# A fused scan and feed-forward kernel: another written order of its opening (loads, weights, early up-projections, PSUM banks)

## The chip, the core and the metric

The kernel runs on one core of a Trainium2 chip. The core has a matrix engine (PE, with its weight loads shown as PEld), a vector engine (DVE), a scalar engine (ACT), a general engine (POOL) and a queue engine (SP) that here only issues DMAs. Each takes its own instructions in order; DMAs are issued from SP, from ACT and from POOL. The metric is the time of one execution on the device in microseconds (us); less is better. The compared number is the median of several executions.

## The reference

Two layers run one after the other. The first is a state-space scan over x (4 batches, 8 heads, 768 steps, 32 wide) with decays a, and B and C (16 states); the second is a feed-forward layer with squared ReLU on the 3072 tokens of 256 features that come out of it.

```python
for c in range(nc):                                   # 24 chunks of 32 steps
    cum = np.cumsum(log(clip(a, 1e-6, 1))[chunk])
    L = np.exp(cum[:, None] - cum[None, :]) * causal
    M = (Cc @ Bc.T) * L                               # scores, masked and decayed
    y[chunk] = M @ xc + (Cc @ state) * np.exp(cum)    # inside the chunk + carried state
    state = np.exp(sum(la)) * state + (Bc * np.exp(cum[-1] - cum)).T @ xc
h = np.maximum(x @ w_in, 0.0)                         # x: y as (3072, 256); w_in (256, 2048)
out = h * h @ w_out                                   # w_out (2048, 256)
```

## The kernel before

The work is cut into twelve units of 256 steps, one per batch and third of the sequence: units 0 to 3 are the first thirds of the four batches, 4 to 7 the second, 8 to 11 the last. Inside a unit the scan is done in two halves of 128 steps. A unit goes through: loads of C, B and x; products with running decay products P and 1/P (`prep_c`, `prep_b`, `prep_x`, lines 152 to 181: C times P and a cast of B into the tile `jt`, x over P into `xs`); a transpose of `jt` on PE (L195) and its copy to `bct` (L208 on ACT, L210 on DVE); scores on PE (`ph_mt`, L220) into PSUM banks 0 to 3; the causal mask on each of the four banks (L229 on DVE directly, or L234, a copy on ACT, and then L238 on POOL or DVE); state products (`ph_u`) and the products inside the unit and with the carried state (`ph_carry`, `ph_intra`; all through the helper's L245); and a copy of the result from PSUM to the tile T (`ph_t`), which is already the transposed input of the feed-forward layer. For the units of the first thirds the state that goes from the first half of the unit to its second is built from PSUM in one instruction, Sd (`ph_sd_first`, L343).

The feed-forward work of a unit is called a block, a to l for units 0 to 11. It has eight up-projections (`mm1`, L403, four matmuls each into one PSUM bank, and L408, the ReLU on ACT), eight squares (L414, on DVE) and eight down-projections (`mm2`, L430, four matmuls each into the block's accumulator in bank 6 or 7). Up-projection f of any block needs the f/2-th of four loads of w_in, down-projection f the f/2-th of four loads of w_out. These eight loads are issued from POOL and convert from 32 to 16 bits on the way (L139, L143).

P comes from a: two loads of 16 KB each for the first thirds (units 0 to 3) and one of 64 KB for the rest, a clip and a scan on DVE (L468, L469), then products on PE that spread the result over partitions (L452, and L521 or L537 for the totals of a half), read from PSUM bank 4 by the first unit and copied to `P_sb` for the others (L688). `Ptot` and `Pquad` (L524, L527) hold the totals. The second and last thirds have a scan of their own (`second_scan`, L468, L469, L532) and products of their own (`second_p`).

The order of all instructions is written out by hand in the string ORDER (lines 48 to 69), token by token; `one` (L655) turns a token into calls, and each engine takes its own instructions in that order. Tokens used below: `fa0`, `fa1`, `la` the loads of a; `ldC0:l:a` a load of C for unit 0, here its first four heads, from ACT's queue (`s` SP; without `l` or `h` all eight heads); `wi0`, `wo0` weight loads; `gB3`, `afC2` instructions on POOL that touch a loaded tile; `ef eb ti ku pi` constants on POOL; `sk` the first scan, `sp` L452, `su` L521, `ps` and `to` the copies of P and of the totals, `fq` L527, `sn`, `p2`, `pq` the same for the other thirds; `pc pb px` the preparations, `tr tc` transpose and copy, `mt` scores, `mk` a direct mask, `sc` and `ms` a copied one, `u` state products, `sf` Sd, `ina inb in` and `ca` products inside and from the carried state, `t` the copy to T, `us` a copy of the state, `zb sb` the state after a unit; `a0` to `l7` up-projections, `qa0` squares, `A0` down-projections; `id3:512` three filler matmuls of 512 columns (L476).

PSUM banks are handed out by `bank` and `pair`, the longest unused one first. Where fillers stand, PE has nothing else to do in that order. DMAs issued from SP and ACT take eight completion semaphores in turn, so a load waits until the one eight places before it has landed.

## Time and profile before

| | |
|---|---|
| median of 3 runs | 116.54 us (116.23 to 118.86) |
| the profiled execution's own time | 116.84 us |
| span of its profile, first to last instruction | 115.1 us |
| PE, PEld, DVE, ACT, POOL busy | 108.9, 93.5, 84.2, 76.7, 49.8 us |
| chain that ended last | PE 87%, DMA 6%, POOL 2% |
| read from memory, written to it | 10.58 MB, 3.15 MB |

The span is what the profile sees of the core; the execution's own time has 1.7 us more around it. PE is busy 95% of the span, but fillers count as busy, and the average hides where the gaps are: the first 17 us and the rest have different limits, so the profile is read by stretches. DMA moves some 190 GB/s from 2.5 to 28 us and much less after that.

### The profile page before, as it was taken

The numbers are of one execution on the slowest core, as the hardware profiler recorded it, in microseconds if no ns is written. First come the engines' busy times: TensorE is split into PE (matmuls) and PEld (weight loads), VectorE is DVE, ScalarE is ACT, GpSimd is POOL, SyncE is SP. The second block draws the span as 40 slices with busy tenths as digits, with TensorE's granted clock in tenths as the row PEclk, the third lists the DMA queues.
The fourth block names the chain that finished last, engine by engine and source line by source line (L and its number), as shares of the span: only waits on it lengthen the run. The fifth ranks groups of instructions, "written<-read, shape, count | busy, mean of one in ns | idle before, by whom it ended". The sixth has DMA issues, their size and how long they took to land.

```text
span 115.1 us, 3998 instructions
## 1 busy us (share of the span) xinstructions
PE 108.9 (95%) x1623; PEld 93.5 (81%) x1623; DVE 84.2 (73%) x187; ACT 76.7 (67%) x161; POOL 49.8 (43%) x102
## 2 busy tenths in 40 slices
PE   7977969999999999999999999999999999999990
PEld 2344749978898989989989989989989899899980
DVE  2469996779599969969965989849668488445530
ACT  0655667865598756787486686786777776876840
POOL 7369972068599457548602669038020020000000
PEclk9999999999999999999999999999999999999999
DMA  1999999989999913935915926623023020020202
GB/s 29 199 196 145 199 203 189 215 167 210 180 191 211 214 24 108 160 89 155 179 46 122 178 97 123 132 95 73 0 100 68 0 100 0 6 91 0 91 0 91
DMA packets 47814, 13.46 MB, mean 117 GB/s; under 512 B 44276, under 2 KB 45876, under 8 KB 47796
## 3 DMA queue, kind: packets, MB, share of 16 engines
q1 hardware_dynamic: 43828, 10.64, 44.8%
q0 software_dynamic: 1664, 2.10, 10.8%
q10 hardware_dynamic: 2304, 0.48, 2.0%
q8 instruction: 12, 0.20, 0.8%
q14 instruction: 6, 0.05, 0.1%
HBM read 10.58 MB, written 3.15 MB: 119 GB/s over the span
## 4 chain that ended last, share of the span: by engine, by line
PE 87%; DMA 6%; POOL 2%; issue 1%; DVE 1%; ACT 1%; ACTq 0%; DVEq 0%
PE pp L430 36%; PE pp L403 36%; PE pp L245 6%; DMA w_out_b<-in_moe_w_out_dram 6%; PE pp L476 4%; PE pp L220 3%; POOL mts L238 1%; PE pp L195 1%; POOL jt L158 1%; PE pp L452 1%; DVE jt L158 0%; DVE Sd L343 0%; ACT bct L208 0%; PE pp L521 0%; ACT osl L722 0%
## 5 line engine op out<-in xcount | busy, mean ns | idle before, releaser
L408 ACT ACTIVATE hb<-pp 128x512 bf16<-128x512 f32 x96 | 55.0, 599 | 24.7 <-PE pp L403 23.1
L430 PE MATMUL pp<-w_out_b,h 128*128 128x256 bf16 (+1 forms) x400 | 54.3, 268 | 0.8 <-DMA w_out_b<-in_moe_w_out_dram 0.8
L414 DVE TENSOR_TENSOR h<-hb 128x512 bf16<-128x512 bf16 x96 | 45.0, 486 | 12.7 <-ACT hb L408 12.3
L403 PE MATMUL pp<-T,w_in_b 128*128 128x256 bf16 x384 | 54.2, 273 | 0.0
L403 PEld LDWEIGHTS <-w_in_b 128*128 128x128 bf16 x384 | 41.4, 114 | 2.2 <-issue 1.0
L430 PEld LDWEIGHTS <-h 128*128 128x128 bf16 x400 | 37.6, 98 | 5.4 <-DVE T L210 1.1
L229 DVE TENSOR_TENSOR mts<-pp,mask 128x512 bf16<-128x512 f32 x45 | 29.6, 677 | 3.3 <-PE pp L220 3.3
L331 POOL TENSOR_TENSOR Sd<-z,Pquad 128x256 bf16<-128x256 f32 x16 | 11.1, 693 | 32.9 <-DVE z L315 25.7
L177 POOL TENSOR_TENSOR xs<-x_nat,Pinv 128x256 bf16<-128x256 f32 (+1 forms) x19 | 14.4, 776 | 5.2 <-DVE Pinv L546 4.6
L158 POOL TENSOR_TENSOR jt<-C_nat,P_sb 128x128 bf16<-128x128 f32 x22 | 9.4, 449 | 1.5 <-ACT P_sb L688 1.0
L476 PE MATMUL pp<-const-bfloat16-1.0 128*128 128x512 bf16 (+2 forms) x19 | 7.3, 516 | 0.8 <-PEq L748 0.8
L315 DVE SCALAR_TENSOR_TENSOR z<-z,Ptot,us 128x64 f32<-128x64 f32 x8 | 2.2, 281 | 6.3 <-ACT us L299 5.4
L437 ACT COPY osb<-pp 128x512 f32<-128x512 f32 x11 | 6.3, 584 | 0.4 <-PE pp L430 0.4
L245 PE MATMUL pp<-mts,xs 64*32 64x128 bf16 x384 | 5.9, 219 | 0.1
L170 POOL CAST jt<-B_nat 128x128 bf16<-128x128 f32 x17 | 5.4, 341 | 1.4 <-DMA B_nat<-in_B_dram 1.4
L220 PE MATMUL pp<-bct 32*64 32x256 bf16 x192 | 5.1, 279 | 0.9 <-DVE bct L210 0.6
L476 PEld LDWEIGHTS <-const-bfloat16-1.0 128*128 128x128 bf16 x19 | 2.2, 122 | 4.0 <-issue 3.7
L245 PEld LDWEIGHTS <-xs 64*32 64x32 bf16 x384 | 4.2, 90 | 0.6 <-issue 0.4
L282 ACT CAST T<-pp 128x512 bf16<-128x512 f32 x7 | 4.1, 592 | 0.4 <-PE pp L245 0.2
L208 ACT CAST T<-pp 128x256 bf16<-128x256 f32 x8 | 2.6, 375 | 2.6 <-PE pp L245 2.6
L245 PE MATMUL pp<-bct,Sd 128*128 128x128 bf16 x40 | 4.2, 220 | 0.0
L220 PEld LDWEIGHTS <-bct 32*64 32x64 bf16 x192 | 2.1, 102 | 2.0 <-issue 0.6
(62 smaller groups left out, 53.4 us busy)
## 6 DMA issues: line engine op xcount, KB each, us to landing
x_nat<-in_x_dram SPq DMA_DIRECT2D x11, 256.0 KB, 3.7
out_dram<-osb SPq DMA_DIRECT2D x11, 256.0 KB, 3.2
B_nat<-in_B_dram SPq DMA_DIRECT2D x11, 128.0 KB, 3.1
C_nat<-in_C_dram SPq DMA_DIRECT2D x11, 128.0 KB, 3.4
w_in_b<-in_moe_w_in_dram POOLq DMA_DIRECT2D x4, 256.0 KB, 6.8
w_out_b<-in_moe_w_out_dram POOLq DMA_DIRECT2D x4, 256.0 KB, 8.2
x_nat<-in_x_dram ACTq DMA_DIRECT2D x2, 128.0 KB, 3.4
bct<-jt SPq DMA_TRANSPOSE x8, 3.6
```

The source lines that it names most:

```text
L158: eng.tensor_tensor(out=_fap(jt[k % 3], 128 + 144 * g, [[384, 2], [32, 4], [1, 16]]), in0=_fap(loaded[k]["C"], 128 * g, [[16, 2], [32, 4], ...
L177: eng.tensor_tensor(out=_fap(xs, 256 * r, [[256, 2 // n], [32, 8], [1, 32]]), in0=_fap(loaded[k]["x"], 32 * r, [[32, 2 // n], [64, 8], [1, ...
L220: nc.tensor.matmul(pp[64 * u:64 * u + 64, q, r * 256:r * 256 + 256], bct[32 * q:32 * q + 32, r, 0, u * 64:u * 64 + 64], _fap(bct[32 * q:32 ...
L229: nc.vector.tensor_tensor(out=live[k]["mts"][:, q].rearrange("p r g i -> p (r g i)"), in0=pp[:, q, :], in1=mask, op=ALU.mult)
L245: nc.tensor.matmul(dst, w, v, start=bool(need), stop=False, skip_group_check=True, **({} if pos is None else {"tile_position": pos}))
L331: nc.gpsimd.tensor_tensor(out=_fap(S_d, 0, [[128, 2], [32, 4], [1, 32]]), in0=_fap(z, 0, [[32, 2], [0, 4], [1, 32]]), in1=_fap(Pquad, 4 * ...
L403: nc.tensor.matmul(pp[:, h, i * 256:(i + 1) * 256], _fap(w, g * w.shape[2] + (o // 2) * 512 + 2 * (o % 2) + i, [[4, 128]]), T[blk][:, g].r ...
L408: nc.scalar.activation(out=hb.rearrange("p i t -> p (i t)"), in_=pp[:, h, :], func=AF.Relu)
L414: nc.vector.tensor_tensor(out=h2, in0=hb, in1=hb, op=ALU.mult)
L430: nc.tensor.matmul(dst, h2[:, i, r * 128:(r + 1) * 128], w_out_b[gi][:, 2 * o + i, c0:c1], start=first, stop=(fp == 7 and i == 1), skip_gr ...
L437: nc.scalar.copy(out=osb, in_=pp[:, 6 if blk == 1 else 7, :])
L476: nc.tensor.matmul(pp[:, h, 0:int(cols)], ones_b[:, 0:128], ones_b[:, 0:int(cols)] if dep is None else dep, start=True, stop=True, skip_gr ...
```

## The change

The order of the first third of the string is written anew; the rest of it, from tr6 on, is as before but for its line breaks. In words:

- C of unit 0 is loaded right behind the two small loads of a, then B, then x; C's and B's halves from ACT and SP at once, both halves of x from SP. The 64 KB of a come after B of unit 1.
- x of unit 1 is issued from ACT, between the cast of B for unit 0 and the copies of its transposes.
- wi0 is issued when POOL has made its constants, wi1 after `fq`, wo0 after POOL's mask for unit 0, wi2 after `px1`, wo1 and wi3 after POOL's mask for unit 1, wo2 and wo3 directly after these. The instructions gB3 and afC2 are gone.
- Six filler matmuls, not eleven, stand ahead of the first products of P (`sp`); others stand behind it.
- Block a's first four up-projections, then block b's first four, come ahead of the first down-projection. Before it was a0 a1 a3 a2 A0 b3 b0 b2 b1.
- The transposes of unit 1, its state products and a0 to a3 have their banks given by hand (`@`).
- Sd of unit 0 is made by four instructions on ACT, one per quarter of its columns, instead of one on DVE. The second scan and its products move behind a6 and b6.

```diff
@@ ORDER @@
     ORDER = """
-        id3:512 fa1:a la fa0:s ku ef ldx0:h:a eb id2:512 ti id1:512 gB3 pi ldB0:l:a hd ldC0:l:a ldB0:h:s ldC0:h:s
-        ldx0:l:a wm jz0:v mb jz1:v ldB1:s id3:512 sk pbh0:a id2:512 pk pbl0:p wi0 sp pc0:v ldC1:s trB0 wi1 su iv1:0:8
-        trC0 tcC0:0:v tcB0:2:a id1:512 tcC0:1:a ps pb1:a to px0:v jz2:v mt0 id1:512 u0:67 ldx1:s pc1:p fq sc0 mk0
-        id1:512 mk0 ms0:p tr1 tc1:1:v sc0 tc1:0:a sf0 mt1 ldB2:s wo0 ldC2:s ms0:v ldx2:s id1:384 in0 ca0 iv:8:16
-        id3:512 px1:p t0:aa id1:256 mk1 a0 a1 mk1 mk1 mk1 u1 ina1 inb1 sn1 us0 sf1 qa0 a3 ldC3:s wi2 fr p2 wi3 ca1
-        qa1 wo1 pc2 pb2:a t1:vv us1 iv:32:64 a2 zb0 qa2 zb1 A0 ldB3:s wo2 ldx3:s b3 qb3 b0 pq b2 b1 tr2 wo3 sb1 qa3
-        qb0 A1 b5 b4 qb1 qb2 qb5 tc2:1:v qb4 tc2:0:a a5 B0 b6 B1 a7 qa5 iv:16:32 px2 a6 mt2 B3 A2 sc2 u2 b7 us2 pb3:a
-        pc3 mk2 qa6 px3 mk2 A5 ms2:v mk2 ld4 qb6 sf2 a4 qa7 B5 pc4 A6 A3 ld5 pb4 ina2 inb2 tr4 ca2 t2:aa tr3 B4 B2
-        tc3:0:a tc3:1:a u3:45 qb7 ld6 ld7 mt3 qa4 B6 mk3 mk3 mk3 mk3 us3 c4 c5 c0 A4 A7 B7 c6 qc0 za3 qc4 c1 qc5 qc6
-        sa3 px4 qc1 pc5 pb5 bk c2 rg4 tr5 C0 mk4 mk4 qc2 c7 qc7 sb0 c3 qc3 d2 d1 C5 za4 afC2 d0 C1 px5 C4 qd2 zb3 C6
-        C3 qd0 d3 C2 mk4 mk4 C7 px6 sa4 rg5 qd3 sb3 pc6 zb4 sb4 pb6 D0 d4 qd1 tr6 mk5 za5 zb5 sa5 sb5 D1 iv:64:96 mk5
...
+        id3:512 fa1:a fa0:s ef jz0:v ldC0:l:a ldC0:h:s eb id2:512 ldB0:l:a ldB0:h:s hd ti ldx0:l:s ldx0:h:s ku pi
+        id1:512 sk wm mb jz1:v ldC1:s ldB1:s la wi0 sp id1:512 pk id1:256 pc0:v iv1:0:8 trC0 pbh0:a pbl0:v ldx1:a
+        id1:384 tcC0:0:v tcC0:1:a trB0 su tcB0:2:a ps px0:v iv:8:16 to mt0 fr fq wi1 ldB2:s ldC2:s ldx2:s u0:67
+        id3:512 sc0 mk0 mk0 ms0:p sf0:a mk0 pb1:a id2:512:0 ca0 ina0 id1:512 inb0 wo0 pc1:v t0:av px1:p id1:512
+        tr1@34 tc1:1:v tc1:0:a jz2:v us0 id1:512 wi2 a0@5 ldC3:s ldB3:s ldx3:s mt1 mk1 mk1 sc1 a1@4 ms1:p mk1 a2@5
+        a3@4 u1@01 sf1 ina1 inb1 ca1 qa0 t1:av us1 wo1 wi3 id1:512 b0 qa1 b1 iv:16:32 qa2 b2 wo2 wo3 qb0 b3 qa3 A0
+        qb1 A1 zb0 qb2 zb1 B0 qb3 B1 a4 sb1 pc2 pb2:a a5 qa4 tr2 b4 qa5 tc2:1:v tc2:0:a b5 qb4 px2 A2 qb5 mt2 sc2 A3
+        u2 us2 mk2 B2 mk2 B3 ms2:v mk2 sf2 a6 sn1 a7 qa6 ina2 inb2 ca2 t2:aa b6 p2 pq qa7 b7 qb6 A4 iv:32:64 qb7 A5
+        B4 pc3 pb3:a px3 ld4 ld5 B5 A6 pc4 pb4 tr4 A7 B6 B7 c0 c1 qc0 tr3 tc3:0:a tc3:1:a c2 qc1 c3 qc2 u3:45 mt3 C0
+        mk3 qc3 C1 mk3 C2 mk3 us3 C3 mk3 za3 sa3 bk c4 c5 qc4 C4 px4 pc5 pb5 ld6 tr5 ld7 c6 qc5 C5 c7 qc6 rg4 mk4 C6
+        qc7 sb0 mk4 C7 zb3 sb3 za4 d0 sa4 px5 d1 mk4 qd0 d2 mk4 qd1 d3 px6 rg5 qd2 qd3 pc6 zb4 sb4 pb6 D0 d4 tr6 mk5
...
 
@@ -336,10 +336,17 @@
         else:
             state[b] = (z, S_d)
 
-    def ph_sd_first(k):
+    def ph_sd_first(k, eng=None):
 
         v, b = live[k], UNITS[k][0]
         S_d = spool.tile([128, 256], BF16, tag=f"Sd{b}0", name=f"Sd{k}_0")
+        if eng is nc.scalar:
+            for q in range(4):
+                nc.scalar.activation(out=_fap(S_d, 32 * q, [[128, 2], [1, 32]]),
+                                     in_=_fap(pp, v["h"][0] * 512 + 256, [[32, 2], [1, 32]]),
+                                     func=AF.Copy, scale=Pquad[:, total(0, b, 0), q:q + 1])
+            v["S"] = [None, S_d]
+            return
         nc.vector.tensor_tensor(
             out=_fap(S_d, 0, [[128, 2], [32, 4], [1, 32]]),
             in0=_fap(pp, v["h"][0] * 512 + 256, [[32, 2], [0, 4], [1, 32]]),
@@ -349,13 +356,18 @@
     turn = list(range(6))
     busy = set()
 
+    forced = []
+
     def bank():
-        h = next(h for h in turn if h not in busy)
+        h = forced.pop(0) if forced else next(h for h in turn if h not in busy)
+        assert h not in busy
         turn.remove(h)
         turn.append(h)
         return h
 
     def pair():
+        if forced:
+            return tuple(bank() for _ in range(2))
         free = sorted((turn.index(h), h) for h in turn if h not in busy)
         two = [(max(i, turn.index(h + 1)), h) for i, h in free if h + 1 in turn and h + 1 not in busy]
         h = min(two)[1] if two else None
@@ -653,6 +665,8 @@
             return live[0]["mts"][:, live[0]["masked"][int(name)]].rearrange("p r g i -> p (r g i)")
 
         def one(t):
+            t, _, at = t.partition("@")
+            forced[:] = [int(c) for c in at]
             f = t.split(":")
             name = f[0].rstrip("0123456789")
             k = int(f[0][len(name):] or 0)
@@ -695,7 +709,7 @@
                 "tc": lambda: trc(k, "", f[1], eng), "tcC": lambda: trc(k, "C", f[1], eng), "tcB": lambda: trc(k, "B", f[1], eng),
                 "mt": lambda: scores(k), "mk": lambda: mask_direct(k) if k < 4 else next_mask(k), "sc": lambda: score_copy(k),
                 "ms": lambda: mask_copied(k, eng),
-                "u": lambda: first_u(k, f[1] if len(f) > 1 else None), "sf": lambda: ph_sd_first(k),
+                "u": lambda: first_u(k, f[1] if len(f) > 1 else None), "sf": lambda: ph_sd_first(k, eng),
                 "ca": lambda: ph_carry(k, live[k]["h"], live[k]["begun"]),
                 "in": lambda: intra(k, ""), "ina": lambda: intra(k, "a"), "inb": lambda: intra(k, "b"),
                 "t": lambda: region_t(k, f[1]), "us": lambda: region_us(k),
```

More of the change, by code (lines that the diff above doesn't have):

```diff
@@ new lines @@
+        mk3 qc3 C1 mk3 C2 mk3 us3 C3 mk3 za3 sa3 bk c4 c5 qc4 C4 px4 pc5 pb5 ld6 tr5 ld7 c6 qc5 C5 c7 qc6 rg4 mk4 C6
+        qc7 sb0 mk4 C7 zb3 sb3 za4 d0 sa4 px5 d1 mk4 qd0 d2 mk4 qd1 d3 px6 rg5 qd2 qd3 pc6 zb4 sb4 pb6 D0 d4 tr6 mk5
+        za5 zb5 sa5 sb5 D1 iv:64:96 mk5 d5 qd4 D2 pb7 d6 qd5 d7 qd6 D3 zb2 e0 qd7 mk5 e1 qe0 sb2 D4 mk5 D5 ld8 pc7 e2
+        qe1 D6 e3 qe2 px7 D7 rg6 e4 qe3 za6 sa6 tr7 zb6 mk6 e5 qe4 sb6 e6 qe5 e7 qe6 mk6 E0 E1 E2 E3 ld9 px8 mk6 f0
+        qe7 E4 f1 qf0 pc8 E5 pb8 E6 mk6 f2 qf1 f3 qf2 E7 rg7 mk7 F0 f4 qf3 za7 tr8 F1 F2 f5 qf4 f6 qf5 f7 qf6 g0 qf7
@@ new lines @@
+        zb7 sa7 sb7 mk7 F3 mk7 F4 pc9 pb9 px9 ld10 g1 qg0 F5 mk7 g2 qg1 F6 g3 qg2 F7 rg8 za8 zb8 sa8 sb8 g4 qg3 G0
+        mk8 tr9 g5 qg4 G1 mk8 g6 qg5 G2 g7 qg6 G3 mk8 h0 qg7 G4 pc10 pb10 px10 ld11 h1 qh0 G5 mk8 h2 qh1 G6 h3 qh2 G7
+        rg9 za9 zb9 sa9 sb9 h4 qh3 H0 mk9 tr10 h5 qh4 H1 mk9 h6 qh5 H2 h7 qh6 H3 mk9 i0 qh7 H4 pc11 pb11 px11 i1 qi0
+        H5 mk9 i2 qi1 H6 i3 qi2 H7 rg10 za10 zb10 sa10 sb10 i4 qi3 I0 mk10 tr11 i5 qi4 I1 mk10 i6 qi5 I2 i7 qi6 I3
+        mk10 j0 qi7 I4 j1 qj0 I5 mk10 j2 qj1 I6 j3 qj2 I7 rg11 za11 zb11 sa11 sb11 j4 qj3 J0 mk11 j5 qj4 J1 mk11 j6
@@ L70 @@
+        qj5 J2 j7 qj6 J3 mk11 k0 qj7 J4 k1 qk0 J5 mk11 k2 qk1 J6 k3 qk2 J7 rg12 k4 qk3 K0 k5 qk4 K1 k6 qk5 K2 k7 qk6
+        K3 l0 qk7 K4 l1 ql0 K5 l2 ql1 K6 l3 ql2 K7 l4 ql3 L0 l5 ql4 L1 l6 ql5 L2 l7 ql6 L3 ql7"""
     WIN = [(0, 2), (2, 4), (4, 6), (6, 8)]
```

10 lines of the change are left out of this document (removed).

## The prediction, made before the result was known

> **What bounds the kernel now.** I read the span in slices of time first, then the chain that ended last, then PE's timeline of the first 18 us, then the loads.
>
> ```profile
> 2.50:6.50 4.00, 4.00 (x18) 1.52 (x16) 1.49 (x5) 2.17 (x5) 2.23 (x7) 1.00 1.05 193
> 6.50:17.00 10.50, 8.18 (x180) 5.46 (x180) 9.86 (x25) 6.22 (x21) 8.74 (x16) 1.00 1.10 185
> 17.00:28.00 11.00, 10.88 (x131) 9.63 (x136) 8.49 (x22) 8.22 (x18) 4.26 (x7) 1.00 1.10 193
> 28.00:112.20 84.20, 84.18 (x1298) 76.34 (x1297) 63.54 (x135) 59.84 (x117) 32.90 (x64) 1.00 0.46 99
> 10.33 6.49 DMA w_out_b<-in_moe_w_out_dram
> ```
>
> Columns of the first four rows: stretch, length, busy time of PE, PEld, DVE, ACT and POOL, granted clock, DMA share, GB/s. PE is busy 10.88 of 11.00 us from 17 to 28 and 84.18 of 84.20 us after that. So nothing behind 17 us can be won except work itself, and no matmul of work goes away here. The end moves only as the point moves at which PE runs without gaps. The last row, of the chain, says what that point hangs on now: PE's first down-projection, A0, waits for weights that are issued at 10.33.
>
> ```profile
> 0.85 4.85 PE L476 MATMUL pp<-const-bfloat16-1.0 128*128 128x512 bf16 x11 [0.85 <-PEq L748]
> 5.63 0.64 PE L452 MATMUL pp<-eye_f,cp 64*64 64x32 f32 x8
> 8.09 0.42 PE L220 MATMUL pp<-bct 32*64 32x256 bf16 x16 [0.24 <-ACT bct L208]
> 11.44 0.93 PE L476 MATMUL pp<-const-bfloat16-1.0 128*128 128x512 bf16 x4
> 12.20 1.03 PE L403 MATMUL pp<-T,w_in_b 128*128 128x256 bf16 x8
> 13.81 0.63 PE L403 MATMUL pp<-T,w_in_b 128*128 128x256 bf16 x4
> 14.36 0.46 PE L452 MATMUL pp<-eye_f,cp 128*64 128x64 f32 x8
> 15.09 0.39 PE L537 MATMUL pp<-pick_p,spread 128*128 128x16 f32 x2 [0.27 <-DVE pick_p L532]
> 15.55 0.60 PE L403 MATMUL pp<-T,w_in_b 128*128 128x256 bf16 x4
> 16.96 0.60 PE L430 MATMUL pp<-w_out_b,h 128*128 128x256 bf16 x4 [0.81 <-DMA w_out_b<-in_moe_w_out_dram]
> ```
>
> Columns: start, length, engine, line, operation. L476 is filler. Before 16.96 PE has done sixteen matmuls of up-projection, a0 to a3 (8+4+4). In the new order the same sixteen come before b0, and b0 opens the gapless part. So the gain is 16.96 minus the new start of b0, less the second chunks' products (L452 and L537 at 14.36 and 15.09), which move behind that point, less new stalls there.
>
> **The change part by part.** First the a path.
>
> ```profile
> 4.68 0.22 DVE L468 TENSOR_SCALAR a_cl<-a_nat 64x128 f32<-64x128 f32 x1 [0.99 <-DMA a_nat<-in_a_dram]
> 4.94 0.42 DVE L469 TENSOR_TENSOR_SCAN cp<-a_cl,const-float32-0.0 64x128 f32<-64x128 f32 x1
> a_nat<-in_a_dram ACTq DMA_DIRECT2D x1, 16.0 KB, 1.6
> a_nat<-in_a_dram SPq DMA_DIRECT2D x1, 16.0 KB, 3.0
> C_nat<-in_C_dram SPq DMA_DIRECT2D x1, 64.0 KB, 3.6
> 6.31 0.49 DVE L158 TENSOR_TENSOR jt<-C_nat,pp 128x128 bf16<-128x128 f32 x2 [0.96 <-PE pp L452]
> ```
>
> The two 16 KB loads of a land 1.6 us after issue on ACT, first in its queue, and 3.0 us on SP, behind the 64 KB load. The new order puts both first, issued with PE's start near 0.8: landed at 2.4. DVE's wait for them ends now at 4.68 and the scan at 5.36, 0.7 later: by the same, 3.15. PE has six fillers ahead instead of eleven: 0.85 + 6 x 0.43 = 3.4, then the eight products of L452, 0.64 (0.7 with the start): P at 4.15 instead of 6.27, **2.1 us sooner**. C follows a in both queues, issued at 1.25. Its landing I bound by 1.6 (a load ahead of the crowd) and 3.6 us (C now, behind other loads in its queue): 2.9 to 4.9. What is ahead of its end is 32 + 128 KB, at 193 GB/s 0.85 us from 2.5 on, so 3.6, below 4.15. B and x of the first unit follow by the same rate at 4.3 and 5.3.
>
> From P to the scores the new order has on its way: L158 0.49, to 4.67; fillers and four transposes, to 5.3; and on ACT the issue of unit 1's x, new there, between the cast of B and the copies.
>
> ```profile
> 5.29 0.82 SPq L125 DMA_DIRECT2D x_nat<-in_x_dram  x1
> 7.67 0.37 ACT L208 COPY bct<-pp 128x256 bf16<-128x256 bf16 x1 [0.67 <-PE pp L195]
> 8.44 0.18 ACT L524 COPY Ptot<-pp 128x8 f32<-128x8 f32 x1
> 8.77 0.25 PE L245 MATMUL pp<-xs,jt 64*32 64x64 bf16 x16
> 8.77 1.22 DVE L229 TENSOR_TENSOR mts<-pp,mask 128x512 bf16<-128x512 f32 x2
> 9.04 0.23 POOL L527 TENSOR_TENSOR Pquad<-Ptot,quad 128x32 f32<-128x32 f32 x1
> 9.24 1.15 POOL L238 TENSOR_TENSOR mts<-sc,mask 128x512 bf16<-128x512 bf16 x1
> 10.18 0.41 DVE L343 TENSOR_TENSOR Sd<-pp,Pquad 128x256 bf16<-128x256 f32 x1
> 11.31 0.28 PE L245 MATMUL pp<-bct,Sd 128*128 128x128 bf16 x2
> 11.43 0.65 ACT L208 CAST T<-pp 128x256 bf16<-128x256 f32 x2 [1.41 <-PE pp L245]
> L408 ACT ACTIVATE hb<-pp 128x512 bf16<-128x512 f32 x96 | 55.0, 599 | 24.7 <-PE pp L403 23.1
> ```
>
> A whole x took SP 0.82 to issue; on ACT the same, 4.7 to 5.5. Behind it wait two copies of 0.37, P_sb and Ptot (0.2 each): bct whole at 6.25, scores at 6.3 (now 8.09), Ptot at 6.45. So the issue gives back 0.3 of the 2.1.
> [...]
>
> Then three masks on DVE (L229, pitch 0.6): 6.7 to 8.55. POOL: Pquad to 6.7, the issue of wi1 (0.73, row below) to 7.5, its mask 1.15 to 8.65. Unit 0's Sd moves from DVE (L343, 0.41) to four ACT instructions; not in the trace, bounded by Ptot's 0.18 and L208's 0.37 each, 0.7 to 1.5; I take 0.9, near the small copies. It ends near 8.1 and hides behind POOL's mask; at 1.5 it would still. Products and T, now half on each engine: T of block 0 at 9.45 instead of 12.08. Transposes of unit 1 and a filler: a0 at 9.8, scores 10.3, a1 10.7, a2 would start at 11.15. The hand-set banks let a3 start once a1's activation has left bank 4, about 12.0; with two banks and activations of 0.6 (L408, its mean) the four up-projections cannot go faster.
>
> Now the weights.
>
> ```profile
> 3.45 0.21 POOL L480 TENSOR_SCALAR_AFFINE_SELECT pick<-pick 128x16 f32<-128x16 f32 x1
> 5.61 1.64 POOL L139 DMA_DIRECT2D w_in_b<-in_moe_w_in_dram  x2 [0.17 <-issue]
> 10.33 0.60 POOL L143 DMA_DIRECT2D w_out_b<-in_moe_w_out_dram  x1
> DMA to landing us min/median/max: 5.5/6.8/7.6
> DMA to landing us min/median/max: 6.5/8.2/8.3
> 14.20 0.84 DVE L532 TENSOR_SCALAR pick_p<-pick,cp 128x16 f32<-128x16 f32 x1
> ```
>
> The two landing rows are those of the four w_in and the four w_out loads; 5.5 is the first load, alone in its queue. wi0 is no longer behind POOL's cast of B: issued at 3.5 (POOL's setup ends at 3.66 now, with one instruction more), landed by 9.0 to 10.3, in time for a0. wi1, which was issued right behind it at 6.52, now stands behind Pquad, at 6.7. It is alone again in POOL's queue, beside x of unit 1 and B, C of unit 2: 5.5 to 6.8 us, 12.2 to 13.5; I take 5.8, near the load that was alone: **12.5**. a2 wants it at 11.15. So **the next late thing is wi1**, and everything behind a2 on PE waits with it: a2 and a3 at 0.44 each (eight matmuls take 1.03, four 0.60) to 13.4, state products and Sd (0.25 and 0.41) to 14.05, the last products 0.28, T 0.4: b0 at 14.8. wo0, issued after POOL's mask at 8.65, lands by 15.2 to 16.9 at 6.5 to 8.2; A0 comes at 14.8 + 4 x 0.44 = 16.5: hidden, or 0.4 late. The other weights leave POOL from 10.3 to 15 by these times and are wanted one after the other from 18 to 26: at up to 8.3 us each, nothing.
>
> The second scan (L468, L469, L532; 0.22 + 0.42 + 0.84, at least 1.5 us of DVE) moves from in front of block 1's T to behind unit 2's Sd; DVE has 2.5 us free in the 11 there. Its products cost PE what they did, 0.85 less the fill of the two groups: 0.5. They may wait for pick_p, 0 to 0.4, and unit 2's transposes for POOL's C product, about 0.25; against this the 0.12 that PE idles there now: 0.35 in all, bounds 0 and 1.0. The 64 KB load of a, moved behind B on SP, is wanted near 24: nothing. B3, no longer held, queues on SP behind x2, with no compute there.
>
> Sum: 16.96 - 14.8 - 0.5 - 0.35 = **1.3 us**. The profiled execution is 116.84 (span 115.1 and 1.7 around it), 0.3 over the median: 115.5 by it, **115.2** against the median 116.54.
>
> **The rivals.** *The weights are no gate.* If wi1 lands by 11.6 (4.9 us after issue, or issued 0.6 sooner), banks and masks set the pace: b0 at 13.9, gain 16.96 - 13.9 - 0.5 = 2.6 without new stalls: 113.9. For it: the first load, alone, took 5.5 with DMA at 193 GB/s beside it. Against it: none of the eight took less.
>
> *The x issue holds ACT.* Issue of a whole x can take far more than 0.82:
>
> ```profile
> 8.36 2.57 SPq L125 DMA_DIRECT2D x_nat<-in_x_dram  x1
> 15.53 5.99 SPq L125 DMA_DIRECT2D x_nat<-in_x_dram  x1
> ```
>
> On SP nothing stands behind it; on ACT the copies, Ptot, and through Ptot wi1. Each us above 0.82 delays all by one. From 2.1 the gain is gone, from 4.4 the kernel is slower by over 2%; at 5.99 it loses 5.2 - 1.3: 120.4. For it: in these rows the queue held other small loads. Against it: by the times above ACT's queue, with a, C and B in it, is nearly drained at 4.7.
>
> *The clock does not come up in time.* Fillers go at a pitch of 0.43 up to 5.1 and of 0.21 (4 in 0.93) at 11.44. With five fewer in front and gaps after them, the slow pitch may last past 9. Six fillers between the states and the products then cost 1.3 more, and up-projections double until it ends: gain gone, 116.5. For it: the fast pitch comes only after 5 us of gapless work. Against it: the granted column is 1.00 throughout, and by the times above PE has about 1 us of gaps up to 9.
> [...]
>
> **How the numbers follow.** Forecast 0.42, 115.2 (its own range, from wi1's 5.5 to 6.8 us, 114.9 to 116.4); no gate 0.32, 113.9; x issue 0.14, 120.4; clock 0.12, 116.5. 2% is 2.3 us, about what a measurement of this kernel can tell from no change: faster is below 114.2, slower above 118.9. Faster 0.32, within 0.54, slower 0.14. The range runs from 113.4 (no gate, and no 0.5 for the moved products) to 117.7 (w_in at 8.3 us, the longest weight load: 115.2 + 2.5); only the x issue, 0.14, lies outside.
>
> **What would show it.** Right: scan's end near 3.2, L452 near 3.5, scores near 6.3, T of block 0 near 9.5, then an idle PE of about 1 us ahead of a2 that w_in ended, b0 near 14.8, no DMA wait at A0. Wrong: no wait at a2 (then 113.9), the ACT issue of x longer than 2 us, filler pitch of 0.43 past 8 us, or a gapless part that isn't: POOL's setup or DVE, which the sum holds free, would then stand as releaser of PE's gaps behind 17.

## The result: 6% slower

The changed kernel takes 123.50 us (median of 4 runs, 123.03 to 126.66) against 116.39 for the kernel before in the same session (4 runs, 115.60 to 118.86). The ratio is 1.062, 95% interval 1.052 to 1.072. The profiled execution took 123.03 us with a span of 121.3. The forecast of 115.2 was wrong, and so was its range. Ratios here and below leave out runs that the chip disturbed, so a ratio can differ a little from that of the medians.

The new lines push the line numbers up: up-projections are now L415, ReLU L420, squares L426, down-projections L442, fillers L488, the first products of P L464; Sd on ACT is L345, on DVE L350.

First PE's timeline of the opening, in the changed kernel; columns as in the prediction.

```profile
3.49 0.64 PE L464 MATMUL pp<-eye_f,cp 64*64 64x32 f32 x8
6.03 0.42 PE L220 MATMUL pp<-bct 32*64 32x256 bf16 x16
7.39 0.60 PE L488 MATMUL pp<-const-bfloat16-1.0 128*128 128x512 bf16 x2 [0.16 <-issue]
10.87 0.51 PE L195 MATMUL pp<-eye_b,jt 128*128 128x128 bf16 x6 [0.93 <-ACT jt L168]
11.43 0.60 PE L415 MATMUL pp<-T,w_in_b 128*128 128x256 bf16 x4
13.28 1.06 PE L415 MATMUL pp<-T,w_in_b 128*128 128x256 bf16 x8 [0.34 <-DMA w_in_b<-in_moe_w_in_dram]
15.15 0.47 PE L245 MATMUL pp<-mts,xs 64*32 64x128 bf16 x32 [0.62 <-DVE Sd L350]
16.36 1.94 PE L415 MATMUL pp<-T,w_in_b 128*128 128x256 bf16 x16 [0.30 <-DVE T L210]
18.13 1.91 PE L442 MATMUL pp<-w_out_b,h 128*128 128x256 bf16 x16
```

The first row of the new path came at 3.49 (forecast 3.5), the scores at 6.03 (6.3). Then unit 1's transposes come 0.93 late, a0 at 11.43 (9.8), a2 at 13.28 behind w_in (12.5), b0 at 16.36 (14.8). A0, at 18.13, waits for no weight. By the prediction's own formula this opening is worth 16.96 - 16.36 - 0.5 = 0.1 us, where the forecast had 16.96 - 14.8 - 0.5 = 1.66. That is 1.6 us less than hoped, but not a loss. The loss is behind it. The next rows are the changed kernel's stretches (length, busy time of PE, PEld, DVE, ACT and POOL, clock, DMA share, GB/s), then two of the kernel before.

```profile
17.00:28.00 11.00, 9.76 (x144) 8.00 (x142) 8.46 (x22) 7.41 (x17) 2.39 (x4) 1.00 0.93 160
28.00:40.00 12.00, 10.34 (x125) 8.67 (x124) 6.21 (x13) 6.80 (x18) 6.54 (x16) 1.00 0.89 170
40.00:60.00 20.00, 17.98 (x329) 15.52 (x330) 17.32 (x37) 13.69 (x30) 13.15 (x24) 1.00 0.59 107
60.00:118.00 58.00, 58.00 (x833) 53.21 (x831) 40.71 (x88) 40.88 (x78) 15.16 (x30) 1.00 0.35 76
```

```profile
28.00:40.00 12.00, 12.00 (x225) 10.61 (x225) 10.58 (x21) 9.12 (x20) 8.99 (x18) 1.00 1.15 204
40.00:60.00 20.00, 20.00 (x356) 17.83 (x355) 16.98 (x36) 13.33 (x28) 11.27 (x23) 1.00 0.48 105
```

PE idles 1.24 us between 17 and 28, 1.66 to 40 and 2.02 to 60, where the kernel before idles 0.12, 0 and 0; from 60 on it is full in both. From 28 to 40 DVE does 6.2 us of work instead of 10.6: it is not overloaded there, it waits for work, and from 40 to 60 it has more to do than before (17.3 of 20 us). What PE waited for, summed over the changed kernel (total, times, longest):

```profile
PE pp L442 <- DVE h L426: 1.9, 3, 1.0
PE pp L195 <- ACT jt L168: 1.6, 2, 0.9
PE pp L245 <- ACT hb L420: 1.3, 1, 1.3
PE pp L245 <- DVE Sd L350: 1.0, 2, 0.6
PE pp L415 <- DMA w_in_b<-in_moe_w_in_dram: 0.3, 1, 0.3
```

Three waits for squares, one for a bank that a ReLU must empty, two for the cast of B. Where they stand, from PE's timeline of the changed kernel:

```profile
21.55 0.51 PE L195 MATMUL pp<-eye_b,jt 128*128 128x128 bf16 x6 [0.64 <-ACT jt L168]
29.09 3.66 PE L442 MATMUL pp<-w_out_b,h 128*128 128x256 bf16 x32
36.16 0.26 PE L245 MATMUL pp<-xs,jt 64*32 64x64 bf16 x16 [1.33 <-ACT hb L420]
36.35 0.42 PE L220 MATMUL pp<-bct 32*64 32x256 bf16 x16
40.91 0.61 PE L442 MATMUL pp<-w_out_b,h 128*128 128x256 bf16 x4 [1.03 <-DVE h L426]
43.38 0.42 PE L220 MATMUL pp<-bct 32*64 32x256 bf16 x16
45.00 0.61 PE L442 MATMUL pp<-w_out_b,h 128*128 128x256 bf16 x4 [0.66 <-DVE h L426]
```

In DVE's own timeline the hole that precedes them, and in POOL's the wait ahead of unit 3's preparation:

```profile
33.90 0.92 DVE L426 TENSOR_TENSOR h<-hb 128x512 bf16<-128x512 bf16 x2 [3.50 <-ACT hb L420]
```

```profile
29.10 0.30 POOL L554 TENSOR_TENSOR Pquad<-Ptot,quad 128x64 f32<-128x64 f32 x1 [7.02 <-ACT Ptot L550]
```

The scores of units 3 and 4 of the kernel before, for comparison:

```profile
29.97 0.42 PE L220 MATMUL pp<-bct 32*64 32x256 bf16 x16
35.42 0.42 PE L220 MATMUL pp<-bct 32*64 32x256 bf16 x16
```

The reading: the new string writes eight down-projections in a row (29.09, 32 matmuls). During them ACT gets no new up-projection and DVE no square and no mask (3.50 us idle), while unit 3's preparation stands behind the second scan that was moved (POOL idle 7.02 us until its Pquad at 29.10; the second experiment below shows that this is not what makes unit 3 late). Unit 3's scores come at 36.35 instead of 29.97, unit 4's at 43.38 instead of 35.42. The masks that DVE could have done in the hole now stand between squares, and the down-projections, no longer far behind their up-projections, wait for those squares. The written order was a buffer, and the reordering used it up. That is a reading of one trace; the experiments test its parts.

The sum closes. From the start of the gapless part to PE's last matmul the kernel before takes 95.2 us (16.96 to 112.18) and the changed one 102.0 (16.36 to 118.36), 6.8 more. It starts 0.6 earlier, which leaves 6.2, and the span grew by 121.3 - 115.1 = 6.2. Of the 6.8, 4.8 is idle time of PE: 4.92 us, with nine waits that sum to 4.88, against 0.12 in one wait. By what they wait for, the nine are 1.90 for squares, 1.33 for the bank, 1.24 at unit 2 (0.64 for the cast, 0.18 for a copy, 0.42 for Sd) and 0.41 for x on POOL. The other 2.0 is busy time, 97.1 against 95.1: some 0.6 for the moved products of the second scan and, as the rest, 1.4 of broken pipelining (an up-projection matmul is on record for 0.27 us and starts 0.11 behind the one before). This last size is borne out by an estimate: four of them take 0.60 and eight 1.04 in the rows above, so a group that starts behind a wait costs 0.16 beside 0.11 per matmul, and eight breaks more than before cost 8 x 0.16 = 1.3.

### The profile page after: what moved, and what is told of

Same layout as the page of the kernel before. It is cut to its first block, busy times and chain, and to the rows that moved or that the text cites. A ratio compares the mean times of both kernels' runs of the same rounds, so it can differ in the third digit from the quotient of the medians.

```text
span 121.3 us, 3991 instructions
## 1 busy us (share of the span) xinstructions
PE 109.6 (90%) x1621; PEld 92.8 (76%) x1622; DVE 84.0 (69%) x188; ACT 78.5 (65%) x166; POOL 49.4 (41%) x98
## 4 chain that ended last, share of the span: by engine, by line
PE 77%; DVE 7%; DMA 5%; ACT 4%; issue 2%; POOL 2%; ACTq 0%
PE pp L442 32%; PE pp L415 31%; PE pp L245 6%; DMA w_in_b<-in_moe_w_in_dram 5%; DVE mts L229 4%; PE pp L488 3%; PE pp L220 3%; ACT hb L420 2%; DVE h L426 2%; POOL xs L177 1%; ACT bct L208 1%; PE pp L195 1%; PE pp L464 1%; DVE Sd L350 1%; POOL Pquad L539 1%
## 5 line engine op out<-in xcount | busy, mean ns | idle before, releaser
L420 ACT ACTIVATE hb<-pp 128x512 bf16<-128x512 f32 x96 | 55.4, 600 | 26.8 <-PE pp L415 25.3
L426 DVE TENSOR_TENSOR h<-hb 128x512 bf16<-128x512 bf16 x96 | 46.0, 494 | 19.3 <-ACT hb L420 19.1
L442 PE MATMUL pp<-w_out_b,h 128*128 128x256 bf16 (+1 forms) x400 | 53.8, 268 | 1.9 <-DVE h L426 1.9
L415 PE MATMUL pp<-T,w_in_b 128*128 128x256 bf16 x384 | 54.5, 273 | 0.7 <-DMA w_in_b<-in_moe_w_in_dram 0.3
L415 PEld LDWEIGHTS <-w_in_b 128*128 128x128 bf16 x384 | 41.2, 114 | 3.5 <-issue 1.4
L442 PEld LDWEIGHTS <-h 128*128 128x128 bf16 x400 | 37.4, 98 | 7.1 <-DVE h L426 2.7
L331 POOL TENSOR_TENSOR Sd<-z,Pquad 128x256 bf16<-128x256 f32 x16 | 10.3, 651 | 34.4 <-DVE z L315 22.9
L158 POOL TENSOR_TENSOR jt<-C_nat,P_sb 128x128 bf16<-128x128 f32 x20 | 8.5, 443 | 0.0
L488 PE MATMUL pp<-const-bfloat16-1.0 128*128 128x512 bf16 (+2 forms) x15 | 6.0, 493 | 1.0 <-PEq L762 0.8
L245 PE MATMUL pp<-xs,jt 64*32 64x64 bf16 x160 | 3.2, 195 | 2.0 <-ACT hb L420 1.3
L170 POOL CAST jt<-B_nat 128x128 bf16<-128x128 f32 x16 | 4.8, 329 | 0.0
L245 PEld LDWEIGHTS <-jt 64*32 64x32 bf16 x160 | 1.8, 89 | 3.8 <-ACT hb L420 1.6
L282 ACT CAST T<-pp 128x512 bf16<-128x512 f32 x6 | 3.5, 585 | 1.0 <-PE pp L245 0.7
L208 ACT CAST T<-pp 128x256 bf16<-128x256 f32 x10 | 3.3, 374 | 1.1 <-PE pp L245 1.0
```

The costliest lines, as they stand in the source:

```text
L158: eng.tensor_tensor(out=_fap(jt[k % 3], 128 + 144 * g, [[384, 2], [32, 4], [1, 16]]), in0=_fap(loaded[k]["C"], 128 * g, [[16, 2], [32, 4], ...
L245: nc.tensor.matmul(dst, w, v, start=bool(need), stop=False, skip_group_check=True, **({} if pos is None else {"tile_position": pos}))
L331: nc.gpsimd.tensor_tensor(out=_fap(S_d, 0, [[128, 2], [32, 4], [1, 32]]), in0=_fap(z, 0, [[32, 2], [0, 4], [1, 32]]), in1=_fap(Pquad, 4 * ...
L415: nc.tensor.matmul(pp[:, h, i * 256:(i + 1) * 256], _fap(w, g * w.shape[2] + (o // 2) * 512 + 2 * (o % 2) + i, [[4, 128]]), T[blk][:, g].r ...
L420: nc.scalar.activation(out=hb.rearrange("p i t -> p (i t)"), in_=pp[:, h, :], func=AF.Relu)
L426: nc.vector.tensor_tensor(out=h2, in0=hb, in1=hb, op=ALU.mult)
```

## The experiments

All medians below stand beside 116.4 to 117.5 for the kernel before on the same chips. In the experiments' sources the changed kernel's lines stand two further down (L417, L422, L428, L444). Some measurements are given as a lag: the start of the n-th matmul of the feed-forward layer, less that of the kernel before, in us. It shows in which stretch time is lost; `after` is the changed kernel, the labels e1 to e18 are those of the expectations below. It also counts scan work that stands at another place in the string: at the 48th matmul the changed kernel has spent 0.7 us less on such work than the kernel before, so little of its 0.91 there is won.

```
n                  16     48     64    112    128    160    176    192    224    780
after           -1.80  -0.91   0.24   1.17   0.50   2.18   3.39   5.30   6.09   6.17
e2               1.05   1.03   1.04   1.35   0.68   1.84   3.06   4.90   5.70   5.78
e8              -0.98  -0.09   1.06   1.99   1.66   2.57   3.52   5.43   6.23   6.31
e12             -0.52   0.37   1.51   2.45   2.11   3.59   4.69   4.69   5.14   5.24
e6              -0.44   0.45   1.59   2.86   4.26   4.77   4.77   4.77   4.77   4.77
e14             -1.95  -1.05  -0.72   1.62   1.59   1.59   1.59   1.59   1.59   1.59
e18             -0.74   0.16   0.50   1.70   1.67   1.67   1.67   1.67   1.67   1.67
```

In the changed kernel the lag grows by 5.6 us between the 128th and the 224th matmul, 32 to 51 us into the span: 3.6 of this are six of its nine waits, the rest is broken pipelining and unit 3's scan work, which the old string has done by the 128th. The theory after the result, M in the expectations, is that the written order of this middle part loses them; its main rival L puts them on the new order of the loads.

### Opening or middle: the halves exchanged

One kernel takes the new string as far as B1 and then the old one, less what has been done.

```diff
 B0 qb3 B1
-a4 sb1 pc2 pb2:a a5 qa4 tr2 b4 qa5 tc2:1:v tc2:0:a b5 qb4 px2
...
+sn1 p2 pc2 pb2:a iv:32:64 pq tr2 sb1 b5 b4 qb5 tc2:1:v qb4 tc2:0:a a5
...
```

> The new order up to and with B1 (eight up- and four down-projections), then all that is left in the order of the kernel before. Theory M (the time is lost in the new order's middle, from unit 2 to unit 4, not in its opening): the opening's lead of 0.9 us at 48 feed-forward matmuls stays, less 0.5 for the second scan's products: 115.5 to 116.5. Rival L (the new loads, the x issue on ACT and the ungated B3 starve the rest): all of these are kept, so at least 121.

The other takes the old string as far as B1 and then the new one.

```diff
 a5 B0 b6 B1
-a7 qa5 iv:16:32 px2 a6 mt2 B3 A2 sc2 u2 b7 us2 pb3:a
...
+iv:16:32 a4 qa4 qa5 px2 A2 mt2 sc2 A3 u2 us2 mk2 B2 mk2 B3
...
```

> The order of the kernel before up to and with B1 (its loads, its weights, its second scan early), then all that is left in the new order. Theory M: the 5 to 6 us lost between 64 and 224 feed-forward matmuls are lost again: 120.5 to 122.5. Rival L: 116.5. Rival S (the second scan, moved behind unit 2, holds unit 3's preparation on POOL until 29.4): it is early here, so 116.5 to 117.5.

Measured: 122.97 us (ratio 1.053, 1.045 to 1.062) and 123.13 (1.059, 1.052 to 1.065). The second is the clean answer. With the old opening untouched it follows the kernel before at +1.0 up to the 64th matmul (a dip of the clock, last section), is +0.7 at the 128th and +5.8 at the end. The loss is in the same place as in the changed kernel, and the two long waits for squares are there again. The wait of 1.33 for a bank is not; three short ones at unit 3's scores, 0.6 us in all, stand near its place. From its waits of PE, and from the timelines of PE and DVE at unit 3:

```profile
PE pp L444 <- DVE h L428: 1.6, 2, 1.0
35.35 0.26 PE L222 MATMUL pp<-bct 32*64 32x256 bf16 x1
34.09 0.91 DVE L428 TENSOR_TENSOR h<-hb 128x512 bf16<-128x512 bf16 x2 [3.56 <-ACT hb L422]
```

So the new middle alone costs about 4.7 us (5.78 less 1.04); the opening and its loads do not cause it. Rival S falls with this: the second scan is early here and POOL does not wait for it, yet DVE has the same hole and unit 3's scores still begin only at 35.35. What makes them late is their place in the string, behind the eight down-projections: the next kernel moves them ahead, and they come at 31.84. The first kernel did not show the reverse, and by its total it is what rival L expects. Its waits of PE say otherwise: 0.57 for the second scan, 0.83 for unit 2's cast of B and 0.59 for a mask stand behind the seam, and in the opening unit 1's transposes wait 1.85 for the cast of B, not 0.93. It lags 6.2 at the 96th matmul, a dip of the clock being part of that. But from there to the end it loses nothing more (6.03), so the old order behind unit 3 is free of the loss.

### What in the middle: three ways to mend it

Unit 3's preparation, transposes and scores moved ahead of the eight down-projections:

```diff
-t2:aa b6 p2 pq qa7 b7 qb6 A4 iv:32:64 qb7 A5 B4 pc3 pb3:a px3 ld4 ld5 B5 A6 pc4 pb4 tr4 A7 B6 B7 c0 c1 qc0 tr3
...
+t2:aa pc3 pb3:a px3 b6 p2 pq qa7 b7 tr3 tc3:0:a tc3:1:a qb6 A4 iv:32:64 qb7 u3:45 mt3 A5 mk3 B4 mk3 ld4 ld5 B5 mk3
...
```

> The new order with unit 3 alone moved: its preparation ahead of the second scan's products, its transposes, scores and masks among b7 to A6 instead of behind c1. Theory M in the form that unit 3's scan stands one block too late, so that the masks of units 3 and 4 meet on DVE: 117 to 119. In the form that the run of down-projections starves ACT and DVE: 121 to 123. Rival L: 123.

Block c's first four up-projections moved among the down-projections:

```diff
-A5 B4 pc3 pb3:a px3 ld4 ld5 B5 A6 pc4 pb4 tr4 A7 B6 B7 c0 c1 qc0 tr3
...
+A5 c0 B4 pc3 pb3:a px3 ld4 ld5 qc0 c1 B5 A6 qc1 c2 pc4 pb4 tr4 A7 qc2 c3 B6 qc3 B7 tr3
...
```

> The new order with c0 to c3 and their squares alone moved, from behind B7 in between A5 and B7. Theory M in the form that eight down-projections in a row leave ACT and DVE without work for 3 us: 118 to 121. In the form that unit 3 stands too late: 122 to 123.5. Rival L: 123.5.

Neither brought the time back: 122.96 us (1.056, 1.047 to 1.064) and 123.51 (1.058, 1.050 to 1.066). The expectations set two forms of theory M against each other, and the results agree with neither alone: the first kernel lies in the range of the form that blames the run of down-projections, the second at the upper end of the form that blames unit 3's place (and at rival L's 123.5). In the first, unit 3's masks came sooner and the wait for a bank is gone, but the lag at 160 is 2.33, no better than the changed kernel's 2.18; then it waited for squares (1.4 us in two waits) and ended at 6.0. One early unit, or four early up-projections, mends one wait and leaves the next. Then only half of the eight down-projections, four held back behind the up-projections of c:

```diff
-B5 A6 pc4 pb4 tr4 A7 B6 B7 c0 c1 qc0 tr3 tc3:0:a tc3:1:a c2 qc1 c3 qc2 u3:45 mt3 C0 mk3 qc3 C1 mk3 C2 mk3 us3 C3 mk3 za3
+B5 pc4 pb4 tr4 c0 c1 qc0 tr3 tc3:0:a tc3:1:a c2 qc1 c3 qc2 u3:45 mt3 A6 mk3 A7 mk3 B6 mk3 B7 mk3 us3 qc3 C0 C1 C2 C3 za3
```

> The new order with four down-projections alone moved: A6, A7, B6, B7 from ahead of c0 to between unit 3's masks, and C0 to C3 behind these. Theory R: the waits of PE for squares at C0 to C3 and c4 go, 1 to 3 us, 120 to 122.5; the two up-projections of lead at unit 4's region stay, and so does the rest. Rival L: 123.5.

Measured: 123.99 us (1.057, 1.030 to 1.085): also missed. Its waits of PE:

```profile
PE pp L444 <- DVE h L428: 1.4, 2, 0.8
PE pp L247 <- ACT hb L422: 1.3, 1, 1.3
```

The wait for a bank is still there, and the waits for squares stand at 41.05 and 45.13, as in the changed kernel. The held four were spent on unit 3's masks, and at unit 4 the string again has up-projections only two ahead of the down-projections. So the same kernel with c4 to c7 written among C1 and C2, five ahead at that point instead of two:

```diff
-us3 qc3 C0 C1 C2 C3 za3 sa3 bk c4 c5 qc4 C4 px4 pc5 pb5 ld6 tr5 ld7 c6 qc5 C5 c7 qc6 rg4 mk4 C6 qc7 sb0 mk4 C7
+us3 qc3 C0 za3 sa3 bk c4 C1 c5 qc4 c6 C2 qc5 c7 qc6 px4 pc5 pb5 ld6 tr5 ld7 qc7 rg4 mk4 C3 C4 mk4 C5 sb0 zb3 sb3 C6 za4 d0 sa4 px5 C7
...
```

> e8 with one more edit: c4 to c7 interleaved with C1 and C2 instead of behind C3, so that five up-projections are ahead of the down-projections when unit 4's region begins, not two. Theory Q (PE waits for squares because the new order lets the lead of up- over down-projections fall to 0 to 2 in front of unit 4's masks): the waits of 0.8 and 0.7 us for squares and the fill behind them go, 120 to 121.7. If the lead is not it: 122.9 to 124.

Measured: 121.91 us (1.042, 1.034 to 1.049), 0.2 above the range of the theory of the lead and 1.0 below that of its rival. No wait for squares is left in it, as that theory says, and from the 128th matmul to the end its lag grows by 3.1 us, not by 4.7 as in e8. So the lead explains the waits for squares, and not all of the loss: with 7, 6, 4 and 5 up-projections ahead at `mt2`, `tr3`, `us3` and `rg4`, near the old string's 10, 6, 3 and 6, it is still 4% slower. These are its longest waits of PE:

```profile
PE pp L247 <- ACT hb L422: 1.5, 2, 1.3
PE pp L197 <- ACT jt L170: 1.4, 2, 0.8
```

Finally the new string as far as b7, with unit 3's transposes there, and the old string behind:

```diff
-t2:aa b6 p2 pq qa7 b7
+t2:aa pc3 pb3:a px3 b6 p2 pq qa7 b7
-qb6 A4 iv:32:64 qb7 A5 B4 pc3 pb3:a px3 ld4 ld5 B5 A6 pc4 pb4 tr4 A7 B6 B7 c0 c1 qc0 tr3
...
+tr3 tc3:0:a tc3:1:a iv:32:64 A5 ld4 qb6 B5 pc4 A6 ld5 pb4 tr4 B4 u3:45 qb7 ld6 ld7 mt3 B6 mk3 mk3 mk3 mk3 us3
...
```

> The new order up to b7 (with its loads, its opening and its unit 2), unit 3's preparation and transposes as in e4, and from there the order of the kernel before: A4, A7, B6 and B7 stay in reserve behind unit 3's scores, and six up-projections are ahead of the down-projections when unit 4's region begins, not two. Theory R (the new middle spends its reserve of down-projections before unit 3's scores take all banks and DVE): 116.5 to 118.5. Rival L (the new loads cost the time): 121 or more. Rival K (whatever is put together from two orders stalls, as e1 did): 121 to 123.

Measured: 121.17 us (1.035, 1.008 to 1.063). It missed the expected time, and by its total alone it could be rival L or K. But the stretch of the loss is clean: the lag is 4.77 from the 160th matmul to the end. What it loses, it loses earlier: a dip of the clock, waits for the cast of B and for Sd, and 0.95 for a bank at 34.72.

### What in the opening: the loads

x of unit 1 back on SP's queue:

```diff
-ldB1:s la
...
-pbl0:v ldx1:a
+ldB1:s ldx1:s la
...
+pbl0:v
```

> The new order with one load moved: x of unit 1 issued from SP behind B of unit 1 instead of from ACT. Rival L in the form that the x queue on ACT delays B of unit 1 (landed at 10.29): B lands by 8, a0 starts 2 us sooner, 121.5. Theory R: the opening may win up to 0.8 us, which the middle's waits then take or leave: 122.5 to 123.5.

Measured: 123.24 us (1.062, 1.045 to 1.079), the same; B of unit 1 landed after 6.6 us, not 6.4. The second queue neither won nor lost anything that can be seen. In the changed kernel the issue on ACT took 0.38, not the 0.82 that the forecast copied from SP:

```profile
4.69 0.38 ACTq L125 DMA_DIRECT2D x_nat<-in_x_dram  x1
10.31 0.50 ACT L168 CAST jt<-B_nat 128x128 bf16<-128x128 f32 x2 [2.02 <-DMA B_nat<-in_B_dram]
```

The second row is what did matter: ACT waits 2.02 us for B of unit 1. That load is issued at 3.93, behind x and C on SP, and lands 6.4 us later. The queues of the changed kernel from 5 to 6.5 us and from 6.5 to 8.5 (packets, MB, share of the engines):

```profile
q1 hardware_dynamic: 1644, 0.21, 111.3%
q0 software_dynamic: 15, 0.02, 15.2%
```

```profile
q0 software_dynamic: 248, 0.24, 87.6%
q1 hardware_dynamic: 334, 0.04, 23.3%
q10 hardware_dynamic: 206, 0.05, 11.7%
```

While wi0's packets of 1 KB (q0) pass, the small packets of 128 B that carry B and SP's other loads (q1) fall from 0.21 MB in 1.5 us to 0.04 MB in 2; the third queue, q10, adds 0.05. Two kernels moved wi0 away from B: one issues it behind `fq`, just ahead of wi1, the other has POOL touch unit 0's B (afB0) before it issues wi0.

```diff
-la wi0 sp
...
-fr fq wi1
+la sp
...
+fr fq wi0 wi1
```

> The new order with one weight load moved: wi0 issued at 7 us, right ahead of wi1, instead of at 3.7. From the packets: while wi0's moved (6.5 to 8.5 us), SP's small packets fell from some 95 to 10 KB per half us, so B of unit 1 should land by 7.5 instead of 10.29, and T of block 0 and unit 1's transposes come 1 to 1.5 us sooner, but wi0 lands near 12.5: a0 at 12.6 instead of 11.4. Total 123 to 124.5 by theory R, since the opening neither wins nor loses over 1 us; by rival L in the form that early weights cost the time, 121 to 122.

```diff
-la wi0 sp
+la afB0 wi0 sp
```

> The new order with wi0 held on POOL until the first half of B of unit 0 has landed, so issued near 5.3 instead of 3.7. Theory P (early weight packets squeeze the small loads): B of unit 1 lands by 8 instead of 10.3, PE's wait of 0.9 at unit 1's transposes goes, a0 starts near 11, b0 0.3 to 1.0 us sooner: 122 to 122.8. Rival (B's landing is the queue's length, not the weights): B lands after 9.5, 123 or more.

Measured: 125.73 us (1.067, 1.038 to 1.096) and 123.23 (1.053, 1.045 to 1.061). B of unit 1 landed after 4.3 and 3.8 us instead of 6.4; here the second, from the view of its tile:

```profile
DMA to landing us min/median/max: 3.8/3.8/3.8
```

So theory P is right about B. But the weights then came later: in the first, a0 waited 1.07 and a2 0.81 for w_in; in the second, a2 waited 2.36. (Both profiled executions, of 127.25 and 127.86 us, hold a dip of the clock from 15 and from 17 us on, see the last section.) In the changed kernel the queues together moved 183 GB/s from 2.5 to 6.5 us and 198 from there to 17; with wi0 moved, B came sooner and a weight later in both runs, and the time did not fall. In the last of this group B and C of unit 2 are prepared before block b, to take away the wait of 0.64 at 21.55:

```diff
-a4 sb1 pc2 pb2:a a5
+a4 sb1 a5
...
-t1:av us1 wo1
+t1:av us1 pc2 pb2:a wo1
```

> The new order with the C product and B cast of unit 2 alone moved, from behind a4 to behind block 1's T. PE's wait of 0.64 at unit 2's transposes (for the cast on ACT, which stands behind a4's activation) and of 0.18 at its scores should go: by theory Q and by all others 0.3 to 1.0 us less than the new order, 122 to 122.8, unless the next wait takes it: 123.

Measured: 123.16 us (1.053, 1.045 to 1.061). That wait was gone, which won 0.8 us between the 48th and the 64th matmul. But the profiled execution had lost 0.9 in the opening (lag -0.02 at the 48th, against -0.91), with 1.28 of wait for B's cast at unit 1's transposes, not 0.93. From the 64th to the 224th it lost the same 5.9 us as the changed kernel. Whether the 0.8 shows in the time can't be told: the ratio is lower, but the intervals overlap.

### A mixed version, and what keeps it back

New string to b7 and old string behind, wi0 held for B, unit 2 prepared early, and banks set by hand at the point where the string of e6 waited for one:

```diff
-c4 c5 c0 A4
+c4@4 c5@5 c0@0 A4
...
```

> e6 (new opening and unit 2, old order from unit 3 on) with wi0 held as in e15, unit 2's preparation early as in e13, and c4, c5, c0 given banks 4, 5 and 0, which unit 3's masks leave first. Theories P and Q: e6 less 0.95 and 0.35 at c4 and c6, 0.6 at unit 2 and 0.5 in the opening: 118 to 119.5. If the waits only move: 120 to 121.5.

Measured: 118.90 us (10 runs, 117.69 to 121.42; ratio 1.010, 1.004 to 1.016). Of the 6% all but 1% is back, by changes of order and three banks alone, with nearly the changed kernel's opening. With e2 this says that most of the loss is in the middle. It has one long wait left behind 17 us, and a strange record on DVE:

```profile
PE pp L222 <- DVE bct L212: 1.5, 1, 1.5
```

```profile
21.00 2.63 DVE L428 TENSOR_TENSOR h<-hb 128x512 bf16<-128x512 bf16 x2 [1.27 <-ACT hb L422]
23.55 0.34 DVE L212 COPY bct<-pp 128x384 bf16<-128x384 bf16 x1
```

One square of the two took 2.30 us, the other its usual 0.41, and a copy that PE needs stood behind them. POOL works without a gap from 19.65 to 23.00 there. Three kernels ask whether the place of the copy or POOL's company is at fault.

```diff
-tc2:1:v tc2:0:a
+tc2:1:a tc2:0:a
```

> The mixed version with one edit: both halves of unit 2's bct are copied by ACT, none by DVE. In the mixed version the DVE copy stood behind a square that took 2.30 us (21.00 to 23.30) and PE waited 1.54 us at unit 2's scores. If the place on DVE is what costs (theory A), the second copy ends near 22.8 on ACT, the wait falls from 1.54 to about 0.5 and the time by about 1 us, to 117.9. If what costs is that DVE itself loses 1.9 us beside POOL (theory B), the square is still near 2.3 us and PE waits for squares or masks a little later instead: 118.5 to 119.

```diff
-mk2 B3 ms2:v mk2
+mk2 B3 ms2:p mk2
```

> The mixed version with one other edit: unit 2's copied mask goes from DVE to POOL, so that POOL must wait for unit 2's scores before it multiplies C and x of unit 3, and does nothing beside the square of DVE from 21.3 to 24.4. If POOL's company stretches the square (theory B), no square there takes more than about 0.9 us, the copy of bct ends near 22.4, the wait of 1.54 falls to 0.2 to 0.5 and the time to about 117.6. If the long record has another cause (theory A: it waits for its input or for a buffer of h), it stays near 2.3 us and the time near 118.9.

The third has both edits.

> The mixed version with both edits: unit 2's bct copied by ACT alone and its copied mask on POOL. Both theories let the wait at unit 2's scores go; 117.3 to 117.8. If the kernel stays at 118.5 or more, the next wait behind has taken the gain, and the trace names it.

Measured: 118.63 us (1.012, 1.006 to 1.018), 117.85 (1.010, 1.004 to 1.016) and 118.46 (1.012, 1.005 to 1.019). The ratio stays at e14's, and the third missed its expected 117.3 to 117.8. The wait at unit 2's scores fell to 0.57, 0.18 and 0.56, as both theories allow; e16 waits 1.19 for Sd next. With POOL's work moved the square was normal (0.49), as theory B says. But against theory B's forecast it was also normal (0.49, the next 0.55) with only the copy moved; there POOL kept its work, began it at another moment and did the last product at 25.51. So the place of the copy is not what stretches the square; that it is a certain overlap with POOL is likely, but which overlap does it these three runs don't show. It can turn up elsewhere: in e18, DVE and then POOL, earlier:

```profile
8.69 2.17 DVE L160 TENSOR_TENSOR jt<-C_nat,P_sb 128x128 bf16<-128x128 f32 x2
10.79 0.41 DVE L212 CAST T<-pp 128x256 bf16<-128x256 f32 x1
```

```profile
8.81 0.61 POOL L145 DMA_DIRECT2D w_out_b<-in_moe_w_out_dram  x1
9.44 1.06 POOL L179 TENSOR_TENSOR xs<-x_nat,Pinv 128x512 bf16<-128x512 f32 x1
```

Two products that take 0.3 each in the changed kernel take 2.17 here; the first of them alone ends at 10.66, as POOL's work ends at 10.50. PE waited 0.77 for it. Behind 17.5 us PE of e18 waits only 0.18, 0.08 and 0.20, so what is left of its lag is in the opening (0.77 here, 0.55 for w_in, 0.72 for a bank, 0.62 for Sd, 0.30 for T) and in the products of the second scan, which were moved behind it. No version tried is faster than the kernel before.

## Why the prediction was wrong

- **The failed step** is the term of new stalls behind b0: "0.35 in all, bounds 0 and 1.0". It measured 6.2 us (4.8 of waits and 1.4 of broken pipelining). The prediction looked there at two edits only, the moved second scan and unit 2's preparation. It took from a PE that is busy 84.18 of 84.20 us that nothing behind 17 could be won, and left out that it could be lost: the string is rewritten as far as unit 5, and the prediction never compared how far the up-projections run ahead of the down-projections in the two strings, nor where unit 3 stands in them. Counted in tokens the lead is 7, 2, 1 and 2 at `mt2`, `tr3`, `us3` and `rg4` in the new string, 10, 6, 3 and 6 in the old. That count needs no run.
- **What is shown of its parts.** The waits for squares (1.90) hang on the lead: e12, which brought the last of the four counts from 2 to 5, lost them. The wait for a bank (1.33) is gone in e4, where unit 3 stands ahead of the run of down-projections; but in e2, with unit 3 behind it, only 0.6 in three waits is left of it, so the place is not its whole cause, and the rest stays open. At unit 2 (1.24), e13 removed the 0.64; the transposes waited there for the cast on ACT, where the forecast had 0.25 for POOL's product. Mending one part alone took 2 of the 6% away at most (e12), and no run mends all of them in the changed kernel itself; the sum of the parts is read from its trace.
- **The second scan's move** was priced at "0 to 0.4" of PE. POOL idled 7.02 us for its Pquad, in front of unit 3's preparation, and the forecast had nothing for that. But the middle's loss doesn't hang on it: e2, where the second scan is early, loses 4.7 us there all the same.
- **The a path** was right: L464 at 3.49 (3.5), scores at 6.03 (6.3), Sd on ACT 0.93 (0.9). T of block 0 was half done at 10.12 on DVE; its other half on ACT stood behind the cast of B and came at 11.08 (9.45).
- **The x issue on ACT** cost 0.38, not 0.82, so its rival fell; e9 shows the choice of queue to be worth nothing that these runs can tell: 123.24 beside 123.50 us.
- **B of unit 1** had no landing of its own in the forecast. It landed 6.4 us after its issue, beside wi0 (4.3 and 3.8 with wi0 moved, e11 and e15), and a0 came at 11.43 instead of 9.8. As a2 still waited 0.34 for wi1, it was wi1 and not this that set a2's start.
- **wi1 as the next late thing** was the right mechanism: issued at 6.97 (6.7) and landed just before 13.28 (12.5), after 6.3 us (5.8). Behind it the forecast had 2.3 us from a2 to b0; it was 3.1. Half of the 0.8 more is the products inside unit 1 (15.15), which stood behind Sd as well and which the forecast left out; another 0.2 is Sd, which PE had after 0.62 us of wait where the forecast had 0.41. So b0 came 1.56 late, and the opening brought 0.1.
- **Small slips** changed nothing: 0.85 us behind 2.5 is 3.35 for C's landing, not 3.6, and a wi1 that lands after 6.8 us gives 116.2 as the upper end, not 116.4.
- **The other rivals**: the weights were a gate, so the first fell. The clock came up in time: two fillers at 7.39 started 0.22 apart, the quick pitch, where the first six had 0.43. The last sentence of the forecast, a gapless part that isn't gapless, names the kind of thing that happened, without a chance or a price.
